# Scores' tails moved to the first head's step, and the attention's output transposed by DMA with GpSimd normalisation

## The chip, the cores and the metric

The kernel runs on one core of one Trainium2 chip. The metric is the device time of one execution in microseconds (us), as the median of the runs. Names of engines in the profile: PE is TensorE's matmul and PEld its weight load, DVE is VectorE, ACT is ScalarE, POOL is GpSimd, SP is SyncE, which here only issues DMAs; SPq is SP's queue of them.

## The reference

The inputs are q, k and v of shape (8 batches, 8 heads, 576 tokens, 64) and two weight matrices, all float32. Attention keeps the 32 largest scores of each row; its output goes through an FFT mix over tokens and channels, and then through an MLP with a residual.

```python
scores = scale * q @ k.transpose(0, 1, 3, 2)
kth = np.partition(scores, -32, axis=-1)[..., -32:-31]
scores = np.where(scores >= kth, scores, -1e9)
attn = np.exp(scores - max); attn = attn / (attn.sum(-1) + 1e-9)
x = (attn @ v) with heads side by side        # (8, 576, 512)
u = x + np.real(fft(fft(x, axis=1), axis=2))
un = (u - mean(u)) / np.sqrt(var(u) + 1e-6)   # over the 512 channels
out = u + np.maximum(un @ w_ch1, 0) @ w_ch2   # 512 -> 2048 -> 512
```

## The kernel before

The order of all work is written out by hand: one loop over steps i (from line 1487), and each step issues instructions to every engine. A step's unit of attention work is an *item*: one head's 128 query rows against all 576 keys (or both heads' 64-row remainders together). A *pair* is two heads of one batch and has 9 items, `IN_PAIR` on line 326: tile 0 of head 0, tile 0 of head 1, tile 1 of each, then the remainders of both heads as one item (t = 4, e = None), then tiles 2 and 3 of each head. A batch has 4 pairs, so 36 items; there are 32 pairs and 288 items in all.

An item passes through these stages, some steps apart:

- Three steps ahead, `scores(j, 0)` multiplies the queries with the first 512 keys. For a first head (e = 0) it does both heads, each in a PSUM tile of its own from the pool `ps_s` (two buffers), which ScalarE copies to the SBUF tile S (L398, L401). The last 64 keys of both heads, the *tails*, are one more matmul, `scores(j, 1)`, with `kt` holding both heads' tail keys (L368) and two small copies (L372). Before the change it is issued in the following step, the one whose item is the second head (e = 1), into another buffer of `ps_s`.
- VectorE finds the 32 largest: four MAX8 (L422) and three MATCH_REPLACE8 (L424) per item.
- GpSimd's `bounds` (L431, tile nt) makes the threshold; ScalarE (L445) and GpSimd (L448) mask, ScalarE takes the exponential and the row sums `den` (L456).
- The weights P must then be transposed. In batch 0 and in pairs 7 and 31 TensorE does it (`transposes`, L524). In the other 26 pairs (`pair_by_dma`) it goes by DMA: ScalarE splits each f32 into two planes of 16-bit halves (L469), SP writes these planes to DRAM (L482, L485), and one step later SP issues a DMA transpose that reads them back as the tile PT, with the halves joined again (`turn`, L503).
- A pair's queries form two *chunks*, `CW` wide: 320 (tiles 0, 1 and the remainder, which is tile 4) and 256 (tiles 2 and 3). When a chunk's PT is there, four steps after its last item in the DMA pairs, `attend` multiplies it with v into the one PSUM tile `o` of `ps_o` (L561), in which channels lie on the partitions.
- `attended` copies o to the SBUF tile xT on ScalarE (L575) and prepares the reciprocals rd of the row sums. A step or more later `to_tokens` transposes xT back to tokens on TensorE, three blocks of 128 for chunk 0 and two for chunk 1 (L601), into a PSUM tile tpx, from which VectorE (L605, L612) writes the product with rd into x. In batch 1 ScalarE does this in place of VectorE (L624).

x is one tile of five 128-row token tiles per batch, with two buffers, so batch b's chunks can only be written once batch b - 2 is stored; until then they wait in the list `pending`.

When a batch's x is complete, the mixing follows: folds on GpSimd (on VectorE for the first and last batch), the DFT over tokens (`dft_tokens`, L752), the one over channels, the statistics, the transposes to channels-first, and then the batch's MLP is put into `queue` as units of TensorE work. T0, on line 1379, is the step from which the mixing is laid out; the steps of the folds, the DFT and the arrival of the MLP follow from it. The loop then fills each step with MLP units: `fixed_cost` estimates TensorE's other work in a step, and `level` chooses how full a step may be so that the queue lasts until the next batch's MLP arrives. So batch b's attention runs beside batch b - 1's MLP, and after the last item only MLP work is left.

Work can also be put into a later step with `at(step, where, fn)`; `where` names a place in the step's order. "pool0" is ahead of `bounds` in GpSimd's order. "load" and "load2" are the last places for SP's DMAs in a step.

Of the kernel before, what the change touches and what calls it, by code (L numbers as in the profile page):

```python
# [73 lines left out]
def kernel(  # L74
# [259 lines left out]
    def scores(i, part):  # L334
# [26 lines left out]
        if part == 1:  # L361

            copy = nc.scalar.copy if i else nc.vector.tensor_copy
            shape, name = [P, NF * P], f"sp_{i}_t"
            sp = ps_s.tile(shape, F32, name=name, tag="sp") if i else bank(shape, name)

            q_end = P * t + rows
            nc.tensor.matmul(  # L368
                sp[:, 0:P], lhsT=qT[:, q_end - P:q_end], rhs=kt_t, start=True, stop=True
            )  # L370
            for h, (s_t, r, _, tails) in enumerate(to):
                copy(out=s_t[r, tails], in_=sp[P - rows:P, TAIL * h:TAIL * (h + 1)])  # L372
            return 0.3
# [196 lines left out]
    def attended(pair, ch, late):  # L570

        o, w = o_of.pop((pair, ch)), CW[ch]
        PT.pop((pair, ch))
        xT = attp.tile([P, CW[0]], F32, name=f"xT_{pair}_{ch}", tag="xT", bufs=4)
        nc.scalar.copy(out=xT[:, 0:w], in_=o[:, 0:w])  # L575
        xT_of[pair, ch] = xT
        den = den_t[pair % 3]
        if ch == 0:
            for h in range(2):
                nc.scalar.copy(  # L580
                    out=den[TH * h:TH * (h + 1), 5:6],
                    in_=den[TAIL + TH * h:TAIL + TH * (h + 1), 4:5],
                )
        c0, n = (0, 6) if ch == 0 else (6, 4)
        rd = small.tile([P, 6], F32, name=f"rd_{pair}_{ch}", tag="rd", bufs=6)

        nc.scalar.activation(out=rd[:, 0:n], in_=den[:, c0:c0 + n], func=AF.Copy, bias=1e-9)
        late.append(lambda: nc.vector.reciprocal(out=rd[:, 0:n], in_=rd[:, 0:n]))
        rd_of[pair, ch] = rd

    def to_tokens(pair, ch, at_once=True):
# [3 lines left out]
            x_of[b] = batp.tile([P, 5, DM], F32, name=f"x_{b}", tag="x", bufs=2)  # L595
        x = x_of[b]
        xT, rd = xT_of.pop((pair, ch)), rd_of.pop((pair, ch))
        shape, name = [P, 4, P], f"tpx_{pair}_{ch}"
        tp = ps_o.tile(shape, F32, name=name, tag="o") if at_once else bank(shape, name)
        for n, t in enumerate(CHUNKS[ch]):  # L600
            nc.tensor.transpose(tp[0:ROWS[t], n, :], xT[:, P * n:P * n + ROWS[t]], ident)  # L601
        cols = slice(P * hp, P * (hp + 1))

        def normalise():
            nc.vector.tensor_tensor(  # L605
# [769 lines left out]
    for b in range(B):  # L1375
        end = PER_BATCH * (b + 1) - 1
        last = b == B - 1
        first, soon = b == 0, b == 1
        T0 = end + (2 if first else 3 if soon else 4 if last else 5)
        if first:  # L1380

            for op in fold_tails(b, nc.gpsimd):
# [66 lines left out]
    def fixed_cost(i):  # L1449

        t = 0.55 if 0 <= i - 2 < N and not by_dma(i - 2) else 0.0
        if i + 3 < N:
            t += {0: 1.04, 1: 0.3, None: 0.9}[items[i + 3][2]]
        ch = chunk_at(i)[1] if i > PER_BATCH + 3 else {4: 0, 8: 1}.get((i - 3) % PER_PAIR)
        t += 0.0 if ch is None else (CW[ch] / 115.0 + 0.14 * len(CHUNKS[ch]))
        if i < N and i % PER_PAIR in (0, 5):
            t += 0.7
        return t + costs.get(i, 0.0)
# [25 lines left out]
    for op in top_ops(0, (0, 1)):  # L1484
        op()
    i, carry = 0, 0.0
    while i < N + 5 or plan or queue or sums:
        now[0] = i
        run(i, "begin")
        pair_of = i // PER_PAIR  # L1490
# [14 lines left out]
            preps.append(lambda: prep("q", pair_of + 1))  # L1505
        if i < N and i % PER_PAIR == 5:
            preps.append(lambda: prep("k", pair_of + 1))
        fixed.append(lambda: scores(j - 1, 1) if e == 1 else scores(j, 0))
        n_mask = 0
        fixed += preps  # L1510

        tok = []

        if pending and pending[0][0] <= i and (
            i < 2 * PER_BATCH + 4 or chunk_at(i)[0] is None
        ):
            _, pp, pc = pending[0]
            if pp // NPB < 2 or pp // NPB - 2 in written:
                pending.pop(0)
                tok.append(lambda: to_tokens(pp, pc, not short))  # L1520
        if not short:
            fixed += tok
        for where in ("pe1", "pe2", "pe"):
# [127 lines left out]
```

## Time and profile before

| What | us |
|---|---|
| median of 3 runs | 1889.86 (1888.66 to 1890.06) |
| the profiled execution, its time | 1882.96 |
| the profiled execution, its span from first to last instruction | 1881.2 |
| mean TensorE clock granted in it, as a share of full speed | 0.955 |

Times by engine, by line and by wait all come from the one profiled execution. A group's row gives the line, the engine, the operation, the tiles written and read, the shape and the count; then the busy time of the group in us and the mean duration of one instruction in ns; then how long the engine stood idle just before these instructions and what ended that. Busy time is the union of the instructions' intervals, so for pipelined instructions it is less than count times duration. A row of a stage gives its length and then, for each engine, its busy time and number of instructions, then the granted clock, the mean busy share of the 16 DMA engines, and GB/s. A row of waits reads "who, which line, waits for whom: us in total, times, longest".

### The profile page before, as it was taken

How to read it: one execution, taken by the hardware profiler on the slowest of the kernel's cores; microseconds unless marked ns; L12 is line 12 of the kernel's file. 1: busy time of each engine (PE TensorE's matmuls, PEld its weight loads, DVE VectorE, ACT ScalarE, POOL GpSimd, SP SyncE). 2: the span in 40 equal slices, each digit the busy share in tenths (PEclk: the TensorE clock that was granted, in tenths of full speed). 3: DMA queues.
4: the chain of work that ended last, by engine and by line, in shares of the span. 5: the costliest groups of instructions: out<-in, count | busy, mean ns of one | idle time of the engine just before them, and what ended most of it. 6: DMA issues, size and time to landing. Idle time of an engine off the chain costs nothing.

```text
span 1881.2 us, 26922 instructions
## 1 busy us (share of the span) xinstructions
PE 1713.1 (91%) x8134; PEld 1086.5 (58%) x8134; DVE 1582.7 (84%) x3301; ACT 1295.7 (69%) x3104; POOL 911.3 (48%) x1278
## 2 busy tenths in 40 slices
PE   5567699889899998989999999999999999999999
PEld 3344364364466654666456665666556655666677
DVE  7999999798899999998899998999999999862110
ACT  6878658576788778777777677777787678652100
POOL 4768643455645356354544465355544465341012
PEclk8887899899899999999999999999999999999999
DMA  5333026651468755585455854685466756440132
GB/s 167 105 96 109 24 60 171 175 138 51 118 155 212 178 125 129 149 214 131 123 144 151 215 128 121 141 229 147 125 155 180 179 133 143 121 117 6 51 110 72
DMA packets 516576, 249.16 MB, mean 132 GB/s; under 512 B 398288, under 2 KB 506448, under 8 KB 516432
## 3 DMA queue, kind: packets, MB, share of 16 engines
q1 hardware_dynamic: 515664, 247.23, 50.7%
q8 instruction: 65, 1.06, 0.2%
q14 instruction: 79, 0.65, 0.1%
q10 hardware_dynamic: 768, 0.21, 0.0%
HBM read 93.63 MB, written 84.74 MB: 95 GB/s over the span
## 4 chain that ended last, share of the span: by engine, by line
PE 66%; ACT 10%; DVE 9%; POOL 7%; issue 3%; DMA 3%; SPq 2%; POOLq 0%; DVEq 0%; ACTq 0%
PE hp L963 24%; PE cp L990 8%; PE o L561 7%; PE sp L398 5%; DVE m L422 4%; PE cw L1160 4%; DVE wk L424 4%; PE yp L752 3%; PE cv L1160 3%; PE cp L1029 3%; POOL wk L448 2%; ACT wk L469 2%; ACT wk L445 2%; PE sp_t L368 2%; ACT S L456 1%
## 5 line engine op out<-in xcount | busy, mean ns | idle before, releaser
L448 POOL TENSOR_TENSOR wk<-S,wk 128x576 f32<-128x576 f32 x288 | 406.7, 1412 | 532.5 <-ACT wk L445 509.8
L422 DVE MAX8 m<-wk 128x8 f32<-128x576 f32 x864 | 626.5, 749 | 6.1
L963 PE MATMUL hp<-unT,w 128*128 128x256 f32 (+1 forms) x2048 | 535.3, 412 | 3.8 <-ACT hT L967 2.6
L963 PEld LDWEIGHTS hp<-unT,w 128*128 128x128 f32 x2048 | 379.4, 192 | 134.5 <-issue 33.4
L424 DVE MATCH_REPLACE8 wk<-m,wk 128x576 f32<-128x576 f32 x576 | 427.4, 742 | 0.0
L469 ACT COPY wk<-S 128x576 uint16<-128x576 uint16 x468 | 288.7, 666 | 0.0
L445 ACT ACTIVATE wk<-S,nt 128x576 f32<-128x576 f32 x288 | 222.5, 773 | 92.6 <-POOL nt L431 91.8
L422 DVE MAX8 m<-S 128x8 f32<-128x576 f32 x288 | 213.9, 743 | 45.1 <-ACT S L372 45.1
L990 PE MATMUL cp<-w,hT 128*128 128x512 f32 x512 | 244.0, 613 | 0.0
L561 PE MATMUL o<-PT,v 128*64 128x256 f32 (+3 forms) x1440 | 203.9, 427 | 21.8 <-DMA PT<-planes 9.9
L967 ACT ACTIVATE hT<-hp 128x320 f32<-128x320 f32 (+1 forms) x256 | 103.4, 408 | 160.2 <-PE hp L963 159.2
L424 DVE MATCH_REPLACE8 wk<-m,S 128x576 f32<-128x576 f32 x288 | 213.5, 741 | 0.0
L456 ACT ACTIVATE S<-wk,nt 128x576 f32<-128x576 f32 x234 | 182.4, 780 | 38.3 <-POOL wk L448 37.3
L398 PE MATMUL sp<-kT,qT 64*128 64x512 f32 (+1 forms) x528 | 181.5, 684 | 12.2 <-ACT means L1348 5.1
L561 PEld LDWEIGHTS o<-PT,v 128*64 128x64 f32 x1440 | 117.0, 157 | 105.7 <-issue 33.8
L401 ACT COPY S<-sp 128x512 f32<-128x512 f32 (+1 forms) x264 | 141.5, 586 | 29.5 <-PE sp L398 28.2
L990 PEld LDWEIGHTS cp<-w,hT 128*128 128x128 f32 x512 | 92.9, 194 | 107.8 <-issue 106.0
L1105 POOL TENSOR_TENSOR hT<-hT 128x512 f32<-128x512 f32 x64 | 81.3, 1274 | 105.1 <-ACT hT L967 91.2
L431 POOL TENSOR_TENSOR nt<-m,cc 128x2 f32<-128x2 f32 x288 | 59.2, 206 | 140.3 <-DVE m L422 139.3
L368 PE MATMUL sp_t<-kt,qT 128*128 128x128 f32 x320 | 70.5, 303 | 43.3 <-ACT S L390 24.4
L368 PEld LDWEIGHTS sp_t<-kt,qT 128*128 128x128 f32 x320 | 55.2, 195 | 92.3 <-ACT S L390 32.4
L1160 PE MATMUL cw<-w,hT 128*128 128x256 f32 x448 | 105.9, 383 | 0.5 <-issue 0.4
(160 smaller groups left out, 2133.1 us busy)
## 6 DMA issues: line engine op xcount, KB each, us to landing
planes<-wk SPq DMA_DIRECT2D x208, 288.0 KB, 2.7
w<-w_parts SPq DMA_DIRECT2D x82, 512.0 KB, 4.7
space<-in_moe_w_ch_dram SPq DMA_DIRECT2D x32, 512.0 KB, 3.7
nat<-in_q_dram SPq DMA_DIRECT2D x128, 64.0 KB, 2.4
v<-in_v_dram SPq DMA_DIRECT2D x64, 128.0 KB, 2.9
out_dram<-x SPq DMA_DIRECT2D x32, 256.0 KB, 2.6
nat<-in_k_dram SPq DMA_DIRECT2D x62, 128.0 KB, 2.9
planes<-wk SPq DMA_DIRECT2D x52, 144.0 KB, 2.7
```

The source lines that it names most:

```text
L368: nc.tensor.matmul(sp[:, 0:P], lhsT=qT[:, q_end - P:q_end], rhs=kt_t, start=True, stop=True)
L398: nc.tensor.matmul(sp[r], lhsT=qT[hd, q_cols], rhs=kT[hd, :], start=True, stop=True)
L422: ops.append(lambda src=src, m8=m8: nc.vector.max(out=m8, in_=src))
L424: ops.append(lambda src=src, m8=m8: nc.vector.match_replace(w, m8, src, NEG))
L445: nc.scalar.activation(out=w, in_=Ssb[i], func=AF.Relu, scale=-FAR, bias=Nt[i][:, 1:2])
L448: nc.gpsimd.tensor_tensor(out=w, in0=Ssb[i], in1=w, op=ALU.subtract)
L456: nc.scalar.activation(out=Ssb[i] if by_dma(i) else w, in_=w, func=AF.Exp, bias=Nt.pop(i)[:, 0:1], accum_out=den_t[pair % 3][:, c:c + 1],)
L469: nc.scalar.copy(out=words[:, half, :], in_=src[:, half, :])
L561: nc.tensor.matmul(o[D * e:D * (e + 1), c0:c1], lhsT=vv[:, c, e, :], rhs=pt[:, NF if c == NF else (NF + 1) * e + c, c0:c1], start=(c == 0) ...
L963: nc.tensor.matmul(hp[:, 0:w], lhsT=w1[:, dt, P * it:P * (it + 1)], rhs=unT[:, dt, 0:w], start=(dt == 0), stop=(dt == NDT - 1),)
L990: nc.tensor.matmul(cp, lhsT=hT[:, it, P * n:P * (n + 1)], rhs=w2[:, it, :], start=(it == 0), stop=(it == NIT - 1),)
L1160: nc.tensor.matmul(dst, lhsT=h()[a][:, kc, :], rhs=rhs_of(kc), start=start and kc == 0, stop=kc == NK - 1, skip_group_check=True,)
```

## The change

It has four parts, the first three for the 26 pairs whose P goes by DMA.

1. The tails' matmul and copies are issued in the first head's step, right behind the heads' own; the second head's step has no scores. Their PSUM tile comes from `ps_t` (tag tp, two buffers), in these pairs used otherwise only by the preparation of q and k. For the remainder item only the pool changes.
2. `attended` makes two copies of o, one for each 16-bit half, and SP writes them to a DRAM tile `oplanes`: one write of 128 x 2 x 256 halves, and for chunk 0 a second one of 128 x 2 x 64. `to_tokens` issues DMA transposes from there straight into x, one of 256 columns and, for chunk 0, one of 128, whose last 64 rows land in rows of x's tile 4 that nothing reads. This is at a new place "turn" at the end of a step, also in steps that have an `attend`. TensorE's transposes and the PSUM tile tpx are gone in these pairs.
3. GpSimd normalises x in place, two steps later, at "pool0": one multiplication with rd for two token tiles, and for chunk 0 one more for the 64-row remainder.
4. The planner's figures follow: `fixed_cost` counts the tails in the first head's step and no transposes, T0 of batches 2 to 6 goes from end + 5 to end + 7, and the loop runs up to two steps longer.

```diff
@@ scores
-            sp = ps_s.tile(shape, F32, name=name, tag="sp") if i else bank(shape, name)
+            if by_dma(i):
+                sp = ps_t.tile(shape, F32, name=name, tag="tp")
+            else:
+                sp = ps_s.tile(shape, F32, name=name, tag="sp") if i else bank(shape, name)
@@ attended
-        xT = attp.tile([P, CW[0]], F32, name=f"xT_{pair}_{ch}", tag="xT", bufs=4)
-        nc.scalar.copy(out=xT[:, 0:w], in_=o[:, 0:w])
-        xT_of[pair, ch] = xT
+        if pair_by_dma(pair):
+            words = attp.tile([P, 2, CW[0]], U16, name=f"ow_{pair}_{ch}", tag="xT", bufs=4)
+            src = o[:, 0:w].bitcast(U16).rearrange("p (s h) -> p h s", h=2)
+            for half in range(2):
+                nc.scalar.copy(out=words[:, half, 0:w], in_=src[:, half, :])
+            to = xT_of[pair, ch] = dramp.tile(
+                [P, 2, CW[0]], U16, name=f"oplanes_{pair}_{ch}", tag="oplanes", bufs=6
+            )
+            nc.sync.dma_start(out=to[:, :, TAIL:], in_=words[:, :, 0:2 * P])
+            if ch == 0:
+                nc.sync.dma_start(out=to[:, :, 0:TAIL], in_=words[:, :, 2 * P:])
+        else:
...
@@ to_tokens
+        cols = slice(P * hp, P * (hp + 1))
+        if pair_by_dma(pair):
+            rows = xT.rearrange("p h s -> (p h) s")
+            nc.sync.dma_start_transpose(
+                out=x[:, 2 * ch:2 * ch + 2, cols].bitcast(U16), in_=rows[:, TAIL:]
+            )
+            if ch == 0:
+                nc.sync.dma_start_transpose(out=x[:, 4:5, cols].bitcast(U16), in_=rows[:, 0:P])
+
+            def normalise_in_place():
+                for t0, nt, n, r in ((2 * ch, 2, 0, P), (4, 1, 4, TAIL))[:2 - ch]:
+                    xs = x[0:r, t0:t0 + nt, cols].rearrange("p t (e d) -> p t e d", e=2)
+                    by = rd[0:r, n:n + 2 * nt].rearrange("p (t e) -> p t e", e=2)
+                    nc.gpsimd.tensor_tensor(
+                        out=xs, in0=xs, in1=by.to_broadcast([r, nt, 2, D]), op=ALU.mult
+                    )
+
+            at(now[0] + 2, "pool0", normalise_in_place)
+            return 0.0
@@ the mixing's steps
-        T0 = end + (2 if first else 3 if soon else 4 if last else 5)
+        T0 = end + (2 if first else 3 if soon else 4 if last else 7)
@@ fixed_cost
+            if by_dma(i + 3) and items[i + 3][2] is not None:
+                t += -0.3 if items[i + 3][2] else 0.3
...
-        t += 0.0 if ch is None else (CW[ch] / 115.0 + 0.14 * len(CHUNKS[ch]))
+        t += 0.0 if ch is None else (
+            CW[ch] / 115.0 + (0.0 if by_dma(i - 4) else 0.14 * len(CHUNKS[ch]))
+        )
@@ the loop over steps
-        fixed.append(lambda: scores(j - 1, 1) if e == 1 else scores(j, 0))
+        if e == 0 and by_dma(j):
+            fixed.append(lambda: scores(j, 0) + scores(j, 1))
+        elif e != 1:
+            fixed.append(lambda: scores(j, 0))
+        elif not by_dma(j):
+            fixed.append(lambda: scores(j - 1, 1))
+        else:
+            fixed.append(lambda: 0.0)
...
-            i < 2 * PER_BATCH + 4 or chunk_at(i)[0] is None
+            i < 2 * PER_BATCH + 4 or chunk_at(i)[0] is None or pair_by_dma(pending[0][1])
...
-                tok.append(lambda: to_tokens(pp, pc, not short))
+                if not pair_by_dma(pp):
+                    tok.append(lambda: to_tokens(pp, pc, not short))
+                else:
+                    at(i, "turn", lambda: to_tokens(pp, pc))
...
-        for where in ("pool", "pool2", "load", "load2"):
+        for where in ("pool", "pool2", "load", "load2", "turn"):
```

More of the change, by code (lines that the diff above doesn't have):

```diff
@@ L573, in attended @@
         PT.pop((pair, ch))
-        xT = attp.tile([P, CW[0]], F32, name=f"xT_{pair}_{ch}", tag="xT", bufs=4)
-        nc.scalar.copy(out=xT[:, 0:w], in_=o[:, 0:w])
-        xT_of[pair, ch] = xT
+        if pair_by_dma(pair):
[10 more added lines that the diff above has]
+        else:
+            xT = attp.tile([P, CW[0]], F32, name=f"xT_{pair}_{ch}", tag="xT", bufs=4)
+            nc.scalar.copy(out=xT[:, 0:w], in_=o[:, 0:w])
+            xT_of[pair, ch] = xT
         den = den_t[pair % 3]
@@ L601, in to_tokens @@
             nc.tensor.transpose(tp[0:ROWS[t], n, :], xT[:, P * n:P * n + ROWS[t]], ident)
-        cols = slice(P * hp, P * (hp + 1))
         def normalise():
@@ L1486 @@
     i, carry = 0, 0.0
-    while i < N + 5 or plan or queue or sums:
+    while i < N + 7 or plan or queue or sums:
         now[0] = i
```

## The prediction

> **What bounds the kernel now.** I read the busy times first, then the busy times by stage, because a share over the whole span hides the stages.
>
> ```profile
> PE 1713.1 (91%) x8134; PEld 1086.5 (58%) x8134; DVE 1582.7 (84%) x3301; ACT 1295.7 (69%) x3104; POOL 911.3 (48%) x1278
> PE 66%; ACT 10%; DVE 9%; POOL 7%; issue 3%; DMA 3%; SPq 2%; POOLq 0%; DVEq 0%; ACTq 0%
> ```
>
> ```profile
> core 0: us, PE busy (x) PEld busy (x) DVE busy (x) ACT busy (x) POOL busy (x), PEclk, DMA share, GB/s
> 480.00:692.00 212.00, 197.19 (x944) 124.46 (x943) 199.35 (x413) 166.27 (x395) 107.97 (x161) 0.97 0.63 159
> 1114.40:1320.00 205.60, 199.16 (x963) 125.62 (x962) 188.66 (x393) 156.02 (x368) 104.13 (x154) 0.98 0.62 156
> 1525.20:1722.00 196.80, 192.74 (x930) 124.64 (x930) 147.47 (x312) 121.78 (x296) 81.56 (x122) 1.00 0.43 109
> ```
>
> The first line is busy time by engine, the second the chain of work that ended last; the stages run from one batch's token DFT to the next. TensorE is busy 93% of the stage at 480 us and 97% of the one at 1114 us; VectorE has 94% and 92%. In the steady stages both are near full, and TensorE ends last (66% of the chain). After 1722 us only batch 7's MLP is left, TensorE alone. So I cost the change as TensorE's work plus TensorE's idle time, and ask afterwards whether another engine becomes later. The list of waits over the span says what the idle time was:
>
> ```profile
> PE sp_t L368 <- ACT S L390: 24.4, 16, 3.6
> PE sp_t L368 <- ACT S L401: 18.7, 13, 6.1
> DVE m L422 <- ACT S L372: 45.1, 21, 6.3
> DVE x L605 <- PE tpx L601: 45.5, 22, 5.8
> POOL wk L448 <- ACT wk L445: 509.8, 228, 7.9
> ```
>
> Columns: us in total, times, longest. The matmul for the scores' tails (sp_t) stands on TensorE until ScalarE has emptied a score buffer; VectorE stands twice: for those tails (L372) and for the transposed output (tpx). These are what the change touches. The last line is GpSimd's slack.
>
> **The change part by part.** It touches 26 of the 32 pairs (4 to 30 without 7). The groups of instructions and the views of single lines give the prices:
>
> ```profile
> L601 PE MATMUL tpx<-ident,xT 128*128 128x128 f32 (+1 forms) x160 | 29.0, 279 | 4.9 <-ACT xT L575 4.8
> L605 DVE TENSOR_TENSOR x<-tpx,rd 128x256 f32<-128x256 f32 x57 | 24.0, 422 | 48.5 <-PE tpx L601 45.5 <-DMA out_dram<-x 0.7
> L612 DVE TENSOR_TENSOR x<-tpx,rd 64x128 f32<-64x128 f32 x28 | 7.6, 272 | 0.0
> L575 ACT COPY xT<-o 128x320 f32<-128x320 f32 x64 | 26.3, 410 | 11.0 <-PE o L561 11.0
> L469 ACT COPY wk<-S 128x576 uint16<-128x576 uint16 x468 | 288.7, 666 | 0.0
> L1132 POOL TENSOR_TENSOR x<-x,ct 128x256 f32<-128x256 f32 x30 | 21.6, 729 | 6.6 <-ACT ct L1130 6.5
> L503 SPq DMA_TRANSPOSE PT<-planes x130: 1294/2426/7786, 253.0 to 1645.8; - x130
> DMA to landing us min/median/max: 3.2/4.6/10.7
> L422 DVE MAX8 m<-wk x864: 727/750/762, 11.5 to 1683.7; 128x8 f32<-128x576 f32 x173
> ```
>
> *TensorE's transposes of the output.* Five per pair, 130 of the 160 at L601. They are pipelined, so I take busy time, not duration: 29.0/160 = 0.181 us each, 23.6 us removed, all on the engine that ends last.
>
> *VectorE's normalisation.* It goes in 23 pairs (batch 1 does it on ScalarE): 46 x 0.422 + 23 x 0.272 = 25.7 us, and most of the 45.5 us wait for tpx. TensorE's and VectorE's gains lie side by side and are not added: per steady batch VectorE loses 4.5 us of work and 5.6 + 8.9 us of waits, TensorE 20 x 0.18 = 3.6 us of work. VectorE falls from 205.6 to about 187 to 191 us, TensorE needs 199.2 - 3.6 = 195.6 us: TensorE stays the later, which is why I count only it.
>
> *Tails one step earlier, into ps_t.* One matmul and two 0.21 us copies move; no DMA, nothing on SP or GpSimd. In the other buffer pair they no longer wait for the copies of the two heads. That pair is used only by the preparation of q and k, in steps 0 and 5 of a pair, which are second-head steps and now have no scores: nobody is in the way. The wait is 43.1 us; 7.6 lie before 235 us, where no pair is touched, leaving 35.5, and 26 of the 28 later pairs are touched: 33.0 us. TensorE then meets ScalarE at the next place, the hidden layer's three banks, 3 units or some 5 us later than now. Bounds 10 and 33; I take 20, as the longest of these waits (3.6 us from L390) are shorter than those 5 us but some of the time will show up at another wait.
>
> *ScalarE.* One f32 copy becomes two uint16 copies read with a step from PSUM. No row shows that form. The nearest, L469 (uint16, step 2, SBUF, 666 ns for 576), has the pace of an f32 copy of the same count (586 ns for 512 at L401), so each half costs what the present copy does: by shape 0.44 us (320) and 0.38 us (256), 0.82 per pair, 21 us in all; from above, twice that if PSUM reads 2 bytes at half pace, 64 us; from below nothing is saved. Against it go 30 of 36 ScalarE multiplications of batch 1 at L624 (8.7 us busy), some 7 us. ScalarE is at 76% of a steady stage and would be at 80%; second chunks are evacuated in a first-head step, which now has all four score copies: about 6.7 us of work (planes 1.3, mask 0.8, exponential 1.0, score copies 1.6, the halves and rd 1.0, hidden layer 1.2) where a step lasts 5.7. It catches up in the next step. I charge 3 us (0 to 15).
>
> *GpSimd.* 52 x 0.729 (the 128x256 of L1132) + 26 x 0.45 (64x127 at L648) = 49.6 us, 7.6 per batch. Its idle time before L448 is 76.6 us in that batch, so it fits. The normalisation stands ahead of the bounds in GpSimd's queue, and behind the bounds wait ScalarE's mask, its exponential and its score copies. It is placed two steps, 11.4 us, after the DMA transpose is issued; the longest landing of the present, larger transposes is 10.7 us. I charge 2 us (0 to 60, see the third case).
> The Trainium skill speaks against this move (SBUF — State Buffer, "SBUF: two separate sides"): GpSimd and a VectorE instruction with two SBUF inputs or in a two-port mode lock a shared port pair, one blocking the other wholly. By it up to 49.6 us could be put on VectorE, and the sum would turn from gain to about nothing. The MAX8 row above never exceeds 762 ns although the 1412 ns subtraction of L448 runs beside it in nearly every step, so I add nothing.
>
> *SP and the DMA engines.* Per pair three writes at 0.56 us (the planes' writes, L482) and three transposes. A present transpose of 9 blocks by 256 rows occupies SP for 2.43 us and one of 9 by 128 rows 1.29; a line through both gives 0.66 us for 2 x 256 and 0.41 for 1 x 256: 3.4 us per pair of 51 us. For the 16 engines two neighbouring slices serve:
>
> ```profile
> 1119.50:1124.70 5.20, 3.28 (x10) 1.26 (x8) 4.53 (x10) 5.09 (x14) 3.72 (x3) 0.98 0.16 57
> 1124.70:1129.80 5.10, 5.10 (x9) 1.97 (x9) 4.41 (x10) 3.86 (x9) 4.16 (x5) 0.68 0.69 174
> ```
>
> The first moved 0.16 x 5.2 = 0.8 us for 296 KB, one write of planes; the second 3.5 us for a write and a transpose, so a transpose of 2304 rows of 256 B takes 2.7 us, one of 512 rows 0.6 and of 256 rows 0.3. With the writes a pair adds 2.5 us, a batch 10: the share goes from 0.62 to 0.68. In the stretch from 1237 to 1284 us it is already over 0.8 and the attention's own transposes would land later; TensorE waited only 9.9 us in all for them, with nearly two steps of slack. In SP's queue the new transpose stands ahead of the next pair of planes' transpose, which waits for its write anyway (199.5 us in 107 waits); the new writes wait for ScalarE's copies, with only the loads of q, k, v and the stores behind them, needed steps later. Charge 0 (0 to 10).
> The skill's DMA: Bandwidth & Descriptors (Specifications) wants at least 512 B per transfer; the tails' rows are 128 B, which only a run can price.
>
> *Two more steps before the mixing.* Batches 2 to 6 deliver their MLP two steps later. In the stage at 1114 us the MLP (L963, L990, L1029, L1160) is 132 us of TensorE, 3.7 per step, so 7.3 us of batch 6's MLP slide behind VectorE's end. Where TensorE is full anyway that costs nothing; where it idled before (stages 480 and 692, 15 us each) it does. 0 to 7.3, taken as 3. The planner's new costs only shift MLP units between steps: nothing, as long as the queue is not empty.
>
> **Sum.** 23.6 + 20 - 3 - 2 - 3 = 35.6, say 36 us off the profiled execution, 1883.0 to 1847. That execution is 6.9 us below the median of the runs, 1889.9, so on the median **1854 us**.
>
> **The rivals.** *Waits move (chance 0.20).* The work goes, but the 20 us of waits reappear at ScalarE, and its charge rises to 12: 23.6 - 12 = 12, 1878 us. For it: ScalarE's 6.7 us step; against: its idle time waits for TensorE (L967, 159 us).
> *GpSimd's queue becomes the bound (0.18, slower).* The normalisation waits for its transpose in front of the bounds, and the mask, planes and scores follow late. With e us per chunk that nobody absorbs, 52 chunks cost 52e; from e = 0.7 the gain of 36 is gone; at 1.2, 62 us go and the time is 1916. For it: two of eight chunks fall into the saturated stretch, and fold steps already hold 5 us of GpSimd work; against: 11.4 us of lead.
> *Nothing changes (0.06).* Gains and charges cancel within 0.2% (3.8 us, about what a measurement of this kernel can tell from none): 1890.
> *Forecast (0.56):* 1833 to 1871, from all of the wait and no charge (23.6 + 33 = 57) to the least of it and ScalarE's full charge (23.6 + 10 - 15 = 19).
>
> **Numbers.** The first rival and the forecast are faster: 0.76; same 0.06; slower 0.18. The range 1833 to 1900 holds the forecast, the first rival, no change and the mild part of the third case.
>
> **What would show it.** Right: L601 with 30 transposes and L605 with 11; the sp_t wait under 12 us; VectorE's wait for L372 well below 45; TensorE's busy time near 1690 and steady stages near 200 us. Wrong: L575's halves over 0.6 us; the GpSimd wait for a DMA on x in the list of waits, with ScalarE's wait for nt (91.8 us now) grown by over 30; steady stages of 205 us or more.

## The result and the profile after

The change is slower: 1892.90 us against 1886.12 in the same sessions (18 runs each), a ratio of 1.0036 [1.0025, 1.0048]. The prediction was 1854, faster; the error is 43 us, 36 forecast as gain and 6.8 (0.0036 of 1886) measured as loss.

The profiled execution of the change has a span of 1890.9 us. Its line numbers have moved: the tails are L371 with their copies L375, the MAX8 is L425, attend L564, the halves' copies L581, the DMA transposes L616 and L620, GpSimd's normalisation L626, TensorE's remaining output transposes L635, and the MLP's products L1062 (cp) and L1193 (cw, cv), which multiply with the weight tile w. First the page's busy times and its chain of work that ended last:

```profile
PE 1696.1 (90%) x8004; PEld 1075.4 (57%) x8004; DVE 1564.8 (83%) x3232; ACT 1303.6 (69%) x3126; POOL 950.3 (50%) x1356
PE 64%; ACT 9%; DVE 8%; DMA 7%; POOL 6%; issue 4%; SPq 2%; POOLq 0%; ACTq 0%; DVEq 0%
```

The 130 transposes left TensorE as announced; its busy time is 17.0 us less, not 23.6. But the span grew by 9.7 us, so TensorE stands idle 194.8 us instead of 168.1. In the chain DMA has gone from 3% to 7%, ScalarE and VectorE have shrunk by a point each. The busy times of the stage that begins with batch 4's token DFT, of the one before batch 7's, and of what is left after that:

```profile
1115.10:1325.60 210.50, 200.74 (x946) 125.40 (x946) 188.70 (x387) 159.84 (x384) 110.58 (x167) 0.97 0.66 166
1536.80:1725.00 188.20, 182.81 (x879) 119.85 (x879) 131.98 (x277) 114.36 (x276) 82.24 (x127) 0.98 0.45 115
1725.00:1890.90 165.90, 161.53 (x717) 118.73 (x716) 19.63 (x47) 21.62 (x53) 24.57 (x33) 1.00 0.21 68
```

Before, the last two of these were:

```profile
1525.20:1722.40 197.20, 193.13 (x932) 124.73 (x934) 147.87 (x314) 121.78 (x296) 81.56 (x122) 1.00 0.43 109
1722.40:1881.00 158.60, 154.51 (x700) 115.76 (x700) 19.56 (x47) 21.58 (x53) 24.51 (x33) 1.00 0.21 71
```

The DMA engines' share rose to 0.66 in the first of these stages, near the forecast 0.68. VectorE's busy time there is 188.7 us, as it was before (188.66 in the stage at 1114.4 us). The forecast 187 to 191 is not met by that: it was counted down from 205.6 us, the stage's length, and so stood for VectorE's work and waits together, and the stage is now 210.5 us, 5 longer. Over the span VectorE's work fell by 17.9 us, forecast 25.7. The last stretch is 7.3 us longer and the stage before it 9.0 shorter: batch 6's MLP has moved behind batch 7's token DFT as far as the prediction had it (0 to 7.3); run e6 below says what that is worth. The waits over the span say where TensorE and VectorE stand, first before, then after:

```profile
ACT wk L445 <- POOL nt L431: 91.8, 74, 4.8
PE o L561 <- DMA PT<-planes: 9.9, 4, 7.5
PE cp L1029 <- DMA w<-w_parts: 5.6, 2, 5.3
```

```profile
POOL wk L451 <- ACT wk L448: 560.5, 229, 10.7
ACT wk L448 <- POOL nt L434: 75.0, 56, 4.8
DVE m L425 <- ACT S L375: 42.5, 17, 5.5
PE cp L1062 <- DMA w<-w_parts: 19.6, 6, 5.4
PE o L564 <- DMA PT<-planes: 18.1, 10, 6.6
PE cw L1193 <- DMA w<-w_parts: 12.9, 5, 4.5
PE sp_t L371 <- ACT S L404: 11.0, 5, 6.9
```

The wait for the tails' buffer has fallen as forecast (sp_t; 13.8 us with the second part that the group below shows). The MLP's weight loads are new: 32.5 us in 11 waits on TensorE, against 5.6 before. The wait for the transposed P (tile PT) has nearly doubled, from 9.9. VectorE's wait for the tails' copies (L375) has hardly moved from 45.1. GpSimd's slack (first line) has grown and ScalarE's wait for the threshold nt has not. The groups:

```profile
L371 PE MATMUL sp_t<-kt,qT 128*128 128x128 f32 x320 | 76.6, 322 | 13.8 <-ACT S L404 11.0 <-ACT S L393 2.8
L626 POOL TENSOR_TENSOR x<-x,rd 128x256 f32<-128x256 f32 (+1 forms) x78 | 41.1, 542 | 2.4 <-DMA x<-oplanes 1.7 <-DVE m L425 0.6
L581 ACT COPY ow<-o 128x320 uint16<-128x320 uint16 (+1 forms) x104 | 37.2, 419 | 12.6 <-PE o L564 12.6
L635 PE MATMUL tpx<-ident,xT 128*128 128x128 f32 (+1 forms) x30 | 5.9, 295 | 4.1 <-ACT xT L590 4.0
```

GpSimd waits 1.7 us for the transposed output in 78 multiplications. A uint16 copy out of PSUM with step 2 costs 419 ns in the mean of both shapes, near the estimate (0.44 and 0.38 us).

### The profile page after: what moved, and what is told of

It reads as the page before. It is cut to its first block, busy times and chain, and to the rows that moved or that the text cites. A ratio compares the mean times of both kernels' runs of the same rounds, so it can differ in the third digit from the quotient of the medians.

```text
span 1890.9 us, 26880 instructions
## 1 busy us (share of the span) xinstructions
PE 1696.1 (90%) x8004; PEld 1075.4 (57%) x8004; DVE 1564.8 (83%) x3232; ACT 1303.6 (69%) x3126; POOL 950.3 (50%) x1356
## 4 chain that ended last, share of the span: by engine, by line
PE 64%; ACT 9%; DVE 8%; DMA 7%; POOL 6%; issue 4%; SPq 2%; POOLq 0%; ACTq 0%; DVEq 0%
PE hp L996 22%; PE cp L1023 8%; PE o L564 8%; PE sp L401 5%; PE cw L1193 4%; PE cv L1193 4%; DVE m L425 4%; DVE wk L427 3%; PE yp L785 3%; DMA w<-w_parts 3%; PE cp L1062 2%; POOL wk L451 2%; PE sp_t L371 2%; DMA PT<-planes 2%; ACT wk L448 2%
## 5 line engine op out<-in xcount | busy, mean ns | idle before, releaser
L425 DVE MAX8 m<-wk 128x8 f32<-128x576 f32 x864 | 627.1, 750 | 6.9
L996 PE MATMUL hp<-unT,w 128*128 128x256 f32 (+1 forms) x2048 | 525.2, 410 | 5.8 <-ACT unT L914 3.6
L425 DVE MAX8 m<-S 128x8 f32<-128x576 f32 x288 | 214.1, 743 | 45.6 <-ACT S L375 42.5
L1023 PE MATMUL cp<-w,hT 128*128 128x512 f32 x512 | 233.0, 597 | 0.0
L564 PE MATMUL o<-PT,v 128*64 128x256 f32 (+3 forms) x1440 | 205.7, 432 | 25.4 <-DMA PT<-planes 18.1
L401 PE MATMUL sp<-kT,qT 64*128 64x512 f32 (+1 forms) x528 | 168.0, 676 | 15.9 <-ACT kT L318 7.8
L564 PEld LDWEIGHTS o<-PT,v 128*64 128x64 f32 x1440 | 118.4, 158 | 103.6 <-issue 42.4
L1193 PE MATMUL cw<-w,hT 128*128 128x256 f32 x448 | 109.5, 393 | 14.8 <-DMA w<-w_parts 12.9
L371 PEld LDWEIGHTS sp_t<-kt,qT 128*128 128x128 f32 x320 | 52.3, 195 | 107.8 <-issue 65.1
L1193 PEld LDWEIGHTS cw<-w,hT 128*128 128x128 f32 x448 | 84.7, 195 | 31.3 <-issue 7.3
```

Of the source, the lines that this page charges most:

```text
L401: nc.tensor.matmul(sp[r], lhsT=qT[hd, q_cols], rhs=kT[hd, :], start=True, stop=True)
L425: ops.append(lambda src=src, m8=m8: nc.vector.max(out=m8, in_=src))
L564: nc.tensor.matmul(o[D * e:D * (e + 1), c0:c1], lhsT=vv[:, c, e, :], rhs=pt[:, NF if c == NF else (NF + 1) * e + c, c0:c1], start=(c == 0) ...
L996: nc.tensor.matmul(hp[:, 0:w], lhsT=w1[:, dt, P * it:P * (it + 1)], rhs=unT[:, dt, 0:w], start=(dt == 0), stop=(dt == NDT - 1),)
L1023: nc.tensor.matmul(cp, lhsT=hT[:, it, P * n:P * (n + 1)], rhs=w2[:, it, :], start=(it == 0), stop=(it == NIT - 1),)
L1193: nc.tensor.matmul(dst, lhsT=h()[a][:, kc, :], rhs=rhs_of(kc), start=start and kc == 0, stop=kc == NK - 1, skip_group_check=True,)
```

## The experiments

All medians are in us; "ratio" is against the kernel before in the same session, whose median was 1885.5 to 1888.7. 0.001 is 1.9 us. By these intervals a difference between two runs' ratios is uncertain by 0.002 to 0.003, some 4 to 6 us either way.

| Run | Edit | Median | Ratio [95%] |
|---|---|---|---|
| e1_tails_only | before + part 1 | 1877.9 | 0.9947 [0.9930, 0.9964] |
| e2_output_only | change without part 1 | 1910.7 | 1.0118 [1.0099, 1.0138] |
| e3_mixing_later | before, T0 two steps later | 1903.6 | 1.0081 [1.0063, 1.0100] |
| e4_write_from_act | change, output's writes from ScalarE's queue | 1898.8 | 1.0059 [1.0040, 1.0078] |
| e5_last_pair_on_pe | change, output of a batch's last pair as before, T0 as before | 1885.7 | 0.9992 [0.9979, 1.0005] |
| e6_later_2_to_5 | e3 without batch 6 | 1899.6 | 1.0058 [1.0042, 1.0075] |
| e7_no_turn_back | e1 without TensorE's 130 transposes | 1871.5 | 0.9919 [0.9897, 0.9940] |
| e8_mixing_one_later | before, T0 one step later | 1906.1 | 1.0102 [1.0085, 1.0119] |
| e9_later_p7_first | e3, products p7 and p3 exchanged | 1891.2 | 1.0026 [1.0014, 1.0038] |
| e10_change_p7_first | change, same exchange | 1878.7 | 0.9955 [0.9939, 0.9971] |
| e11_tails_p7_first | e1, same exchange | 1876.8 | 0.9946 [0.9927, 0.9966] |
| e12_no_turn_on_pool | e7, normalisation on GpSimd | 1866.3 | 0.9896 [0.9877, 0.9915] |
| e13_no_normalise | e10 without GpSimd's multiplication | 1879.9 | 0.9959 [0.9944, 0.9974] |
| e14_no_dma | e10 without the output's DMAs | 1863.9 | 0.9878 [0.9854, 0.9902] |
| e15_last_pair_p7_first | e5, same exchange | 1890.6 | 1.0018 [1.0004, 1.0032] |
| e16_change_p7_one_later | e10, T0 one step later, not two | 1890.5 | 1.0024 [1.0009, 1.0039] |
| e17_writes_only | e10 without the DMA transposes | 1872.4 | 0.9922 [0.9908, 0.9937] |
| e18_small_dmas | e10, the output's DMAs cut to a few bytes | 1874.1 | 0.9927 [0.9911, 0.9943] |

**The parts alone.** e1 has the tails' three places of the diff and nothing else; e2 has everything else.

> Only the first part of the change: the tails' matmul and copies in the first head's step, their PSUM tile from ps_t, and the planner's 0.3; the output is transposed on TensorE as before, T0 stays at end + 5. If the prediction's largest wait term was right and the loss comes from the other parts, the sp_t wait falls from 43 us to under 15 and the time is 10 to 25 us below the kernel before (1861 to 1876). If freed waits only reappear at ScalarE, the sp_t wait falls as well but the time stays within 4 us of the kernel before. If the tails' move itself is the harm, it is 5 us or more above.

> All of the change but its first part: the output goes by DMA and GpSimd, T0 at end + 7; the tails stay in the second head's step and in ps_s. If the tails' move gains and the output's path loses, this is the slowest of all, 15 to 30 us above the kernel before (1901 to 1916), with TensorE's waits for w and PT as in the changed kernel. If the output's path is neutral and the tails are the harm, it is within 4 us of the kernel before. The prediction's own sum for it was 16 us below.

The tails alone gain 10 us, the rest loses 22; together the change loses 7, so the two don't simply add. In e1's list of waits the wait for the tails' buffer and VectorE's wait for their copies both fall; others grow:

```profile
DVE m L425 <- ACT S L375: 7.8, 3, 4.0
DVE x L608 <- PE tpx L604: 60.1, 24, 6.7
PE o L564 <- DMA PT<-planes: 24.4, 8, 6.4
PE sp_t L371 <- ACT S L404: 8.8, 5, 4.8
```

VectorE now waits for tpx 60.1 us instead of 45.5, and TensorE for PT 24.4 instead of 9.9: of some 71 us of waits that are gone, 29 turn up at other places.

**The later mixing.**

```diff
# e3 (e8: end + 6; e6: batch 6 keeps end + 5), in the kernel before; the loop's bound follows
-        T0 = end + (2 if first else 3 if soon else 4 if last else 5)
+        T0 = end + (2 if first else 3 if soon else 4 if last else 7)
```

> Only T0 of batches 2 to 6 at end + 7 instead of end + 5 (and the loop's bound). The prediction charged 3 us (0 to 7.3), all of it behind VectorE's end. If the later mixing is what turned the result, this alone is 8 us or more above the kernel before; if it is a minor term, 0 to 7 us above, with the stretch after the last batch's token DFT longer by 5 to 8 us.

> The kernel before with T0 at end + 7 in batches 2 to 5 only; batch 6 keeps end + 5, so its MLP arrives as before. Two theories of the 17 us that the later mixing costs. That they are batch 6's MLP slid behind VectorE's end: the time falls back to within 4 us of the kernel before and the stretch after the last batch's token DFT to 159 us. That the later place hurts in every batch, because the loads of w come to stand beside other loads: 6 to 10 us above the kernel before remain, with TensorE's waits for w at 15 us or more (5.6 us before, 23.7 us with all batches later).

> The kernel before with T0 of batches 2 to 6 at end + 6, one step later instead of two. If the cost grows with the steps (MLP work that slides behind VectorE's end), 6 to 10 us above the kernel before. If it is a collision of the loads of w with the loads of q, k and v that only the second step brings about, 0 to 5 us above, and TensorE's waits for w stay under 10 us.

Two steps later costs 15 us in a kernel that is otherwise the one before, and one step costs more, 19. That batch 6 keeps its place saves only 4 (e6 is 11 us above the kernel before, where 6 to 10 were expected). So most of it isn't work that slides, which would grow with the steps and lie in batch 6. TensorE's timeline shows a part of what it is. Before (start, length, line, count, idle time before it):

```profile
1262.34 2.00 PE L1160 MATMUL cw<-w,hT 128*128 128x256 f32 x8
1265.65 2.91 PE L561 MATMUL o<-PT,v 128*64 128x320 f32 x20 [1.32 <-DVE x L1118]
1268.49 0.49 PE L368 MATMUL sp_t<-kt,qT 128*128 128x128 f32 x2
1268.91 1.94 PE L1029 MATMUL cp<-w,hT 128*64 128x512 f32 x8
```

The same place in e3:

```profile
1272.24 1.89 PE L1160 MATMUL cw<-w,hT 128*128 128x256 f32 x8
1273.97 0.38 PE L368 MATMUL sp_t<-kt,qT 128*128 128x128 f32 x2
1274.29 1.07 PE L1029 MATMUL cp<-w,hT 128*64 128x512 f32 x2
1280.48 3.67 PE L1029 MATMUL cp<-w,hT 128*64 128x512 f32 x6 [5.12 <-DMA w<-w_parts]
```

The last cw group is the MLP's seventh product, p7, the last reader of half of a weight tile that `bring(B21)` then loads again, and cp multiplies with that half next. Before, an attend (2.9 us) and a short wait happened to stand between them while the load ran. At the new place nothing does, and TensorE stands 5.1 us. The stretches of e3 around the stall show a second price:

```profile
1275.40:1280.40 5.00, 0.00 (x0) 0.00 (x0) 4.96 (x10) 2.12 (x5) 1.55 (x2) 0.79 1.16 313
1280.40:1284.20 3.80, 3.72 (x8) 0.88 (x8) 3.73 (x8) 0.00 (x0) 0.00 (x0) 0.50 1.09 214
```

The granted clock behind the stall is 0.50, and 6 matmuls take 3.67 us where 8 took 1.94. The Trainium skill (TensorE: Matmul & The Clock Gate, Part 1 on the HAM clock gate) says that the clock falls to half after at least one idle window of about 3.4 us; the rows agree, with a mean of 0.79 over the 5.0 us of the stall and 0.50 behind it. If the load is the cause, it is enough to issue it earlier. The exchange does that: p7 goes ahead of p3, which then covers the load.

```diff
-        for f in (p2, p1, p5, p4, p6, p3, p7) for part
+        for f in (p2, p1, p5, p4, p6, p7, p3) for part
```

> T0 at end + 7 in the kernel before, as in that run, and the last two of the seven products of the MLP's fast part in the other order (p7 ahead of p3). p7 is the last reader of the half of w2 that is then loaded back; with p3's 3.6 us behind it, TensorE has work while that load is under way. Theory that the later mixing costs its 17 us because nothing stands between p7 and the matmuls that need the load: TensorE's waits for w fall from 24 us to under 12 and the time falls by 6 to 14 us, to 1890 to 1898. Rival, that the later place costs by MLP work behind VectorE's end or by the planner: the time stays within 4 us of 1904, whatever the waits do.

> The changed kernel with the same exchange of p7 and p3. By the theory of the load behind the last product its waits for w fall from 32 us to under 15 and the time by 6 to 15 us, from 1893 to 1878 to 1887, below the kernel before. By the rival it stays within 4 us of the changed kernel.

> The tails' move alone with the same exchange. Its waits for w are only 3.7 us, because an attend stands behind p7 at the old T0. By the theory there is nothing to win here: within 4 us of the tails alone (1874 to 1882), or slower, as p7 now needs its own load and its mix 3.6 us sooner. A gain of 6 us or more would say that the exchange helps for another reason.

The exchange takes 10 us off e3 and 15 off the change, and nothing off e1 (0.9946 against 0.9947), where the mixing stands at the old place. TensorE's waits for w fall with it, from 23.7 us in e3 to 8.1 in e9 and from 32.5 in the change to 11.1 in e10. In e10 cp's part, the load behind p7, is nearly gone:

```profile
PE cw L1193 <- DMA w<-w_parts: 8.2, 2, 4.7
PE cp L1062 <- DMA w<-w_parts: 2.9, 3, 1.4
```

With this one line the change is faster than the kernel before. It is no faster than the tails alone. The load doesn't explain e8: there TensorE waits 19.9 us for w, less than in e3, and VectorE 65.8 us for tpx (45.5 before). Why one step costs more than two stays open.

**What the removed work is worth.** e7 is e1 with VectorE reading xT directly, untransposed, in the 26 pairs: TensorE's 23.6 us go, no other work is added, and the values of x are others. e12 gives those multiplications to GpSimd at "pool0" as well (in batch 1 ScalarE's too), so that both engines are relieved without a DMA.

```diff
# e7, in to_tokens (e12: nc.gpsimd in place of nc.vector)
+        if pair_by_dma(pair):
+            tp = [xT[:, P * n:P * n + P] for n in (0, 1, 0)]
...
-                in0=tp[:, 0:2, :].rearrange("p t (e d) -> p t e d", e=2),
+                in0=(
+                    xT[:, 0:2 * P].rearrange("p (t e d) -> p t e d", t=2, e=2) if pair_by_dma(pair)
+                    else tp[:, 0:2, :].rearrange("p t (e d) -> p t e d", e=2)
+                ),
...
```

> The tails moved, as in the run with that part alone, and the five transposes of each of the 26 pairs left out with nothing in their place: the normalisation reads the untransposed xT, so x holds wrong values. It prices TensorE's 23.6 us by themselves, without DMA, GpSimd or T0. If TensorE's work is worth its full length, the time is 18 to 30 us below the tails alone (1848 to 1860). If something else sets the pace of the steps and TensorE only fills them, it is less than 10 us below (1868 or more).

> The tails' move, TensorE's transposes of the output left out in the 26 pairs, so that x holds wrong values, and the normalisation of the untransposed xT on GpSimd at the same step, at pool0; no DMA, T0 at end + 5. It takes off both TensorE's 23.6 us and VectorE's 25.7 us. Against the same with VectorE (1871.5): if VectorE had become the bound there, 5 to 20 us below it (1852 to 1867); if GpSimd's 41 us in front of the bounds cost as much as they free, within 4 us of it; if GpSimd's queue is what eats the gain of the new output path, 5 us or more above.

Without 23.6 us of TensorE work e7 is 0.0028 or 5 us faster than e1; with VectorE relieved too e12 is at 0.0051, 10 us. The first is not a clean price, since e7 makes VectorE's work longer. Its multiplications, with xT from SBUF and with tpx from PSUM (ns min/median/max):

```profile
L611 DVE TENSOR_TENSOR x<-xT,rd x46: 383/426/1604, 507.6 to 1645.9; 128x256 f32<-128x256 f32 x46
L611 DVE TENSOR_TENSOR x<-tpx,rd x11: 425/425/426, 56.5 to 1700.3; 128x256 f32<-128x256 f32 x11
```

The 46 take 28.8 us instead of some 19.4, and VectorE is busy 9.4 us longer than in e1 (1592.6 against 1583.2). One of the slow ones and GpSimd's instruction beside it (start, length):

```profile
559.22 1.60 DVE L611 TENSOR_TENSOR x<-xT,rd 128x256 f32<-128x256 f32 x1
559.13 1.41 POOL L451 TENSOR_TENSOR wk<-S,wk 128x576 f32<-128x576 f32 x1 [1.29 <-ACT wk L448]
```

VectorE's ends 0.28 us after GpSimd's. In the same way all twelve that take over 0.5 us overlap a GpSimd instruction of 1.3 to 1.4 us and end 0.27 to 0.29 us after it; where GpSimd is idle they take 0.38 to 0.43 us. e7's stage at 895 us has little room left on either engine:

```profile
895.40:1099.10 203.70, 197.17 (x946) 123.83 (x945) 194.91 (x407) 158.75 (x382) 105.22 (x157) 0.98 0.63 161
```

TensorE and VectorE are busy 97% and 96%. In e12 VectorE has 189.0 us in a stage of 203.5 at the same place, and the stage is no shorter. I read this as a chain from TensorE to ScalarE to VectorE and back without slack; no run shows that by itself, and e7 and e12 differ by no more than the error.

**Where the output path's gain goes.** First SP's queue and GpSimd were in question. In e4 the writes go to ScalarE's queue; in e5 the last pair of each batch, the one that forces T0 back, keeps TensorE's transposes.

```diff
# e4
-            nc.sync.dma_start(out=to[:, :, TAIL:], in_=words[:, :, 0:2 * P])
+            nc.scalar.dma_start(out=to[:, :, TAIL:], in_=words[:, :, 0:2 * P])
... (the second write likewise)
# e5: used in place of pair_by_dma for the output; T0 is end + 5
+    def out_by_dma(pair):
+        return pair_by_dma(pair) and pair % NPB != NPB - 1
```

> The changed kernel, with the writes of the output's two halves issued from ScalarE's queue, where they need not wait in SP's queue for ScalarE's copies; bytes, transposes and landing are the same. Theory that SP's queue is the harm (the write waits for ScalarE in front of the loads of w and the planes' transposes, 50 us of SP waits at that line): TensorE's waits for w fall from 32 us to under 15 and the time is 5 to 15 us below the changed kernel (1878 to 1888). Rival, that it is the load of the DMA engines and SP's issue time of the added transposes: the waits for w stay at 25 us or more and the time is within 4 us of the changed kernel.

> The changed kernel with T0 back at end + 5: the last pair of each batch is transposed and normalised as before (TensorE, VectorE), so 20 pairs take the new output path instead of 26. If the later mixing is the harm and the rest adds up with the tails' gain of 9 us, the time is 5 to 20 us below the kernel before (1867 to 1882). If the output's path costs by itself, it is above the tails alone by 3 us or more (1881 or more); if its 18 us of TensorE work pay, below them by 5 us or more (1873 or less).

> The version with the last pair of each batch's output on TensorE as before and the mixing at the old place, now with p7 and p3 exchanged. If the weight load behind p7 is what the place cost, this changes little at the old place, 1878 to 1886 (it measured 1885.7 without the exchange); if the output path by DMA is worth the 10 us of the version without transposes in the pairs that keep it, 1868 to 1876.

> The change with p7 and p3 exchanged and the mixing one step later than before instead of two. If only the load behind p7 made the place matter, within 4 us of 1878.7. If each step of delay still costs what it frees, 3 to 8 us below.

ScalarE's queue is no better a place: e4 is 0.0023 above the change, in neither of its expected ranges. e5 comes out level with the kernel before, so 21 pairs by DMA (not the 20 of the expectation: five of the 26 are a batch's last) lose what the tails gain (0.0045, 8 us). With the exchange (e15) it is not faster but 5 us slower, though TensorE waits only 3.0 us for weight loads in it; e16, in which the fold of the remainders reads the last pair's part before it is normalised, is at 1.0024 although the weight waits are 9.2. Both were expected lower. The place of the mixing costs by more than the load behind p7; in e16 TensorE's idle time that GpSimd ended is 19.8 us against 11.8 in e10, 10.2 of it in two waits of cw for GpSimd's x (L1165), but no run takes that apart.

Four runs then take e10 apart. e13 leaves x unnormalised. e14, e17 and e18 let GpSimd multiply a tile of weights by rd, so that the count and shape of its work stay and the output's values are others.

```diff
# e13
-                    nc.gpsimd.tensor_tensor(
-                        out=xs, in0=xs, in1=by.to_broadcast([r, nt, 2, D]), op=ALU.mult
-                    )
# e14, e17, e18: in0 = w1[0:r, 0, 0:nt * P]; e14 issues no DMA of the output,
# e17 the writes alone, e18 this in their place:
-            nc.sync.dma_start(out=to[:, :, TAIL:], in_=words[:, :, 0:2 * P])
+            nc.sync.dma_start(out=to[0:1, 0, TAIL:P], in_=words[0:1, 0, 0:P - TAIL])
... (the second write likewise, 128 B)
-            nc.sync.dma_start_transpose(
-                out=x[:, 2 * ch:2 * ch + 2, cols].bitcast(U16), in_=rows[:, TAIL:]
-            )
... (the second transpose goes too)
+            for n in range(4 if ch == 0 else 2):
+                s0 = 0 if n > 1 else TAIL
+                few = small.tile([1, 32], U16, name=f"few_{pair}_{ch}_{n}", tag="few", bufs=8)
+                nc.sync.dma_start(out=few, in_=xT[0:1, 0, s0:s0 + 32])
```

> The change with p7 and p3 exchanged, but without GpSimd's multiplication (x stays unnormalised in the 26 pairs). If the 41 us that GpSimd spends in front of the bounds eat the gain: 5 to 12 us below the 1878.7 of the change with the exchange, and ScalarE's wait for nt falls by 10 or more. If the DMAs or the later place eat it: within 4 us of 1878.7.

> The change with p7 and p3 exchanged, but without the writes to DRAM and the DMA transposes of the output: GpSimd multiplies a fixed tile of weights by rd instead (the output's values are others), ScalarE's two copies stay. If SP's and the DMA engines' load eats the gain: 5 to 12 us below 1878.7, near the 1866.3 of the version without transposes, and TensorE's wait for PT under 10 us. If GpSimd or the place eats it: within 4 us of 1878.7.

> The change with p7 and p3 exchanged; the writes of the output's halves to DRAM stay, the DMA transposes that read them back are left out (GpSimd multiplies a fixed tile of weights by rd instead, so the output's values are others). If the transposes are what costs: within 4 us of the 1863.9 without any of these DMAs. If the writes, their issue or SP's wait for ScalarE's halves cost: 1873 to 1880. If both share it: about 1871.

> The change with p7 and p3 exchanged; each write of the output's halves is a write of 128 B in its place, each transpose two reads of 64 B that wait for the same write, so that SP is occupied and blocked much as before while the DMA engines move next to nothing (GpSimd multiplies a fixed tile of weights by rd, so the output's values are others). If SP's queue is what costs: 1875 to 1882. If the DMA engines' work, or its meeting with the other transfers, costs: within 4 us of 1863.9.

GpSimd's multiplication costs nothing that shows (0.9959 without, 0.9955 with it). The output's DMAs cost 0.0077, 14.5 us, more than the 5 to 12 expected, and without them TensorE's wait for PT stays at 15.1 us (16.5 in e10) where under 10 was expected. The writes without the transposes cost 8 of these, and DMAs that move next to nothing 9. So by the medians more than half of it is not bytes; it comes with small issues on SP that wait for ScalarE's halves or the write's landing. That their place in SP's queue is the cause is not shown: e4 takes the writes off that queue and is no faster. What they occupy of SP shows in e10's answer on the tile oplanes (ns min/median/max):

```profile
L585 SPq DMA_DIRECT2D oplanes<-ow x52: 533/565/1376, 295.9 to 1645.5; - x52
L616 SPq DMA_TRANSPOSE x<-oplanes x52: 1192/1250/3651, 300.1 to 1654.5; - x52
L587 SPq DMA_DIRECT2D oplanes<-ow x26: 612/625/1517, 296.5 to 1618.5; - x26
L620 SPq DMA_TRANSPOSE x<-oplanes x26: 1137/1234/1247, 301.5 to 1635.6; - x26
```

By medians that is 29.4 + 65.0 + 16.3 + 32.1 = 143 us of SP, 5.5 per pair. In e18 it is 70 us, with nearly the same cost as the 46 us of e17's writes, so occupied time alone is not the measure either. The remaining 5 to 6 us, no more than the error, come with the transposes at full size, which occupy SP longer and load the DMA engines; the runs don't part the two.

Where the delay arrives can be read from VectorE's wait for the tails' copies, in the lists of waits of e14, e17 and e10:

```profile
DVE m L425 <- ACT S L375: 23.7, 12, 3.9
```

```profile
DVE m L425 <- ACT S L375: 33.1, 15, 3.9
```

```profile
DVE m L425 <- ACT S L375: 40.7, 17, 4.0
```

It rises in the order of the medians (1863.9, 1872.4, 1878.7), and it is 33.0 in e18. ScalarE in turn waits longer for the heads' scores from TensorE (42.4, 53.4 and 55.2 us, and 55.4 in e18). This is where it shows; by which delayed transfer it begins is open, since the present transposes of P land as before (median 4.7 us in e10, 4.6 before).

## Why the prediction was wrong

The sum was -20 (tails), -23.6 (TensorE's transposes) and +8 of charges. The runs give, as differences of ratios times 1886: -10 for the tails (e1), -13 for the output off TensorE and VectorE, with ScalarE's and GpSimd's added work and the later mixing but without DMAs (e14 against e11), +14.5 for the DMAs (e10 against e14), +15 for the place of the mixing that the exchange mends (the change against e10). Together +7, as measured; but these runs lie on one path from the kernel before to the change, so the sum closes by itself and does not test the parts, each of which is uncertain by some 4 to 6 us.

*"Two more steps before the mixing", taken as 3, 0 to 7.3.* This is the first step that failed. I priced it as work that slides, batch 6's 7.3 us of MLP, and asked neither which load lies behind which product nor what else stands between them. The slide is there, 7.3 us in the last stretch, but batch 6 has only 4 of the cost (e6). Alone the later mixing costs 15 us (e3), and it is mostly a collision at a place: an order in which the load is issued earlier takes 10 us of it away (e9). One step costs more than two (e8), which neither the slide nor this load explains. The list of waits before had the line, 5.6 us in 2 waits at L1029; I did not read it as a near miss. That a new batch's MLP stands elsewhere among the attention's work was in the change; that this is harmless was assumed.

*"SP and the DMA engines", charge 0, 0 to 10.* The second. The transposes' price on SP came from a line through two larger shapes, 0.66 and 0.41 us; they took 1.25 and 1.23, and SP 5.5 us per pair instead of 3.4. The DMA engines' share was right, 0.66. That the queue had slack was argued from SP's waits, without asking what lies behind a DMA that has to wait. The runs put 14.5 us on these DMAs; by which way stays open.

*"TensorE's transposes", 23.6 us at full length.* The third. I counted them whole because TensorE was to be the later engine by 4.6 us or more per stage (195.6 against 187 to 191). That sets TensorE's work without its waits against VectorE's work with waits, and takes only the larger as if the engines didn't wait for each other. Both were above 90%; 23.6 us off TensorE were worth 5 (e7, with 9.4 us more on VectorE), relief of both 10 (e12), and e14 gives 13, with the later mixing and ScalarE's second copy against it.

*"Tails one step earlier", 20 of 10 to 33.* The mechanism held and the wait fell nearly as said, from 43.1 to 13.8 (under 12 was the sign); its worth is 10, at the low end, while VectorE's wait for tpx grew by 15 us and TensorE's for PT by 14 (e1). VectorE's wait for the tails, forecast well below 45, fell to 7.8 in e1 and is back at 42.5 in the change; 17 us of it come with the DMAs (23.7 in e14, 40.7 in e10).

*The rivals.* "GpSimd's queue becomes the bound" had the right sign and the wrong mechanism: GpSimd waits 1.7 us for its transposes, ScalarE's wait for nt fell from 91.8 to 75.0, and without the multiplication nothing is gained (e13). "Waits move" describes e1, at half its size and with tpx and PT in ScalarE's place. The Trainium skill's rule of the shared port pair (SBUF — State Buffer, "SBUF: two separate sides") is for VectorE instructions with two SBUF inputs or in a two-port mode. MAX8 reads one tile (m<-wk), so its row, which I held against the rule, doesn't test it. e7's rows agree with it: the multiplication takes up to 1604 ns beside GpSimd with both inputs in SBUF, and at most 426 with one in PSUM. In the change the rule costs nothing that shows: without GpSimd's added work e13 is no faster, and VectorE is busy 1564.5 us there against 1565.0 in e10. The skill's rule for transfers under 512 B (DMA: Bandwidth & Descriptors, Specifications) was left to a run, but none prices the tails' 128 B rows alone; since e18 has 9 of the 14.5 us with next to no bytes, at most the rest can lie there.

What was right: 30 transposes at L635, the DMA engines' share, ScalarE's halves at 419 ns, GpSimd's work in its slack, TensorE's 1696 us of busy time (near 1690). Of the signs of being wrong one came: the steady stages are 206.7 us or longer (205 was the bound).

## What to carry to other kernels

Where an order is written out by hand, moving a block by some steps is not free even if the work is the same: look up which loads are issued by the block's last readers, what covers them now by chance, and let the load's last reader come earlier (one exchanged pair was worth 15 us here, and nothing where the cover was still there). Work taken off the busiest of two engines above 90% should not be counted at its full length until a run with that work left out says more; here 25 us off each were worth some 10 (e12). Such a run must not make other work dearer, as e7 did. A DMA that replaces work on a busy engine has a price too (14.5 us here, mostly not in bytes): count its issues at the duration of the smallest such row, and ask what lies behind it in order. Of the versions with the right output the tails' move alone is the best, 0.9947 of the time before (0.9946 with the exchange); e10, at 0.9955, is level with it.

## What the runs showed of the hardware

The small DMA transposes of e10 occupied SP for 1.23 us (one block of 128 columns by 256 rows) and 1.25 us (two blocks) by their medians, while the present ones, of up to 9 blocks by 256 rows, have a median of 2.5 us there: from two blocks to one the time hardly shrank. The stall of TensorE in e3 cost more than its length: after 5.1 us idle the granted clock was 0.50 for the next 3.8 us, and the matmuls there took 0.61 us each instead of 0.24. ScalarE's reading of every second uint16 from PSUM went at the pace of an f32 copy: 433 and 404 ns for 320 and 256 elements, against 439 and 381 ns for f32. A VectorE multiplication with both inputs in SBUF took 0.4 us beside an idle GpSimd and up to 1.6 us beside a busy one (e7).
